# A spectral filter beside a gated MLP on one core: filter squares, a leftover row's chain and four butterflies stand elsewhere in the background list, and the last token block is split over two PSUM tiles

## Chip, core and metric

The kernel runs on one core of one Trainium2 chip. The metric is device time in microseconds, the median of several executions. Matmuls run on TensorE (PE), elementwise work on VectorE (DVE) and ScalarE (ACT), a few sums over partitions on GpSimd (POOL). Every DMA is issued from SyncE's queue (SP).

## What is computed

```python
xn = _layernorm(x, axis=-1)                      # x: 1 x 2048 x 448
return x + _A_ref(xn, A_w_r, A_w_i) + _B_ref(xn, B_W_gate, B_W_up, B_W_down)

def _A_ref(x, w_r, w_i):
    X = rfft2(x, axes=(-2, -1))                  # 2048 x 225
    X = X * (w_r + 1j * w_i)
    return irfft2(X, s=(S, D), axes=(-2, -1))

def _B_ref(x, W_gate, W_up, W_down):             # 448 -> 1792 -> 448
    gate = jnp.einsum("bsd,df->bsf", x, W_gate)
    up = jnp.einsum("bsd,df->bsf", x, W_up)
    h = gate * (gate > 0) * up
    return jnp.einsum("bsf,fd->bsd", h, W_down)
```

## The kernel before

The 2048 tokens stand as 16 blocks n2 of 128, four blocks to a chunk q of 512. Every f32 operand of a matmul is split into a high and a low float16 part, and a product is three matmuls (high by high, high by low, low by high) into one PSUM bank.

**The MLP is the foreground.** 56 `gu` units (14 slices f of the hidden dimension by 4 chunks) multiply the chunk by the slices of W_gate and W_up into a PSUM tile "gu" of two banks, of which there are two buffers. Units go in pairs: the last 64 input rows of both stand together as four half passes (L738), which also open the second unit's buffer. `gu_post` then follows on each unit: relu on ACT (L768, to g1), times up on DVE (L772), the high part on ACT (L776, to h), the low part on DVE (L780). A gu buffer is free when its L772 is through. `dn` units multiply h by W_down, block by block, into PSUM "dn" (two buffers, L799); DVE adds the result to the output tile xy (L805).

**The filter is the background.** The row DFT over d, the DFT over tokens (128 points by matmul, 16 points by four radix-2 stages on DVE), the product with the filter, and the way back. `stage2`, `stage3`, `stage4` are butterflies over tiles y of 128x456 (L404 to L428); with sign -1 they belong to the inverse. `i_swap`, `i_pair` and `i_quad` undo the pairing of frequencies (a swap of partitions by two DMAs, L529 and L530, into one of four tiles sw; L535 and L536; L602 to L607). `i_hi` and `i_lo` split into vt (L614 on ACT, L620 on DVE), `i_sdft` (L630) and `i_ddft` (L649) are the two inverse DFTs on PE into PSUM "fx" (two buffers), and `i_acc` (L654) adds to xy.

**The filter's scale and the leftover row.** The filter is scaled by a power of two taken from its sum of squares: `wsq` squares the 16 filter tiles on ACT (L186), `wneg` flips signs in them first (L496), `wsq_fin` sums them on DVE (L463) and over partitions on POOL (L189), `wsq_scale` makes the scale fsc on DVE (L192, L196, L470 to L472). Partition 64 of every tile holds two frequencies that don't fit the pairing. It is collected as a 16-row tile "row" and goes its own way: `row_hi`, `row_lo`, `row_dft(0)`, `row_mul`, then `row_hi2` (L566, ACT, needs fsc), `row_lo2` (L570, DVE), `row_dft(1)` (L575, PE), `row_ev` (L588, DVE). `i_swap` puts each row back into its block by a DMA (L592).

**What sets the order.** The foreground's units stand in a fixed list. The background is a list `bg` of items with a DVE cost; after each unit `run_bg` takes as many as the unit leaves room for on DVE. A scheduler then orders each engine's queue by its own model of time, so an item that moves in `bg` moves others on all engines. Each queue is fixed at build time, and each engine works through its queue in order: an instruction that waits holds up all behind it.

In `bg`, the loop over `i0` handles the inverse's first part: filter load, forward stage 4, pair, product (`wmul`), then `back`, which adds the inverse's first butterflies. The next loop, over t, handles one block of the inverse after another. `dn_tail` does the last four token blocks.

Of the kernel before, what the change touches and what calls it, by code (L numbers as in the profile page):

```python
# [10 lines left out]
F32 = mybir.dt.float32  # L11
# [3 lines left out]
OP = mybir.AluOpType  # L15
AX = mybir.AxisListType

S, D, F = 2048, 448, 1792
# [5 lines left out]
GROUPS = [5, 5, 4]  # L24
# [120 lines left out]
def tile_gfnet_reglu(ctx: ExitStack, tc: tile.TileContext, x, xr, wgu, wd, wf, ident, c_fd, c_fm, c_im, c_row, c_id,  # L145
                     out):
    nc = tc.nc
    V, A, P, G = nc.vector, nc.scalar, nc.tensor, nc.gpsimd

    main = ctx.enter_context(tc.tile_pool(name="main", bufs=1))  # L150
    psum = ctx.enter_context(tc.tile_pool(name="psum", bufs=1, space=bass.MemoryType.PSUM))

    def mt(shape, dt, name, bufs=1):
        return main.tile(shape, dt, name=name, bufs=bufs)

    def fx():
        return psum.tile([128, 512], F32, name="fx", bufs=2)
# [18 lines left out]
    dsc = mt([128, len(GROUPS)], F32, "dsc")  # L176
# [365 lines left out]
    def row_wf():  # L542
        w = state["roww"] = it([128, 2 * GW], F32, "roww")
        h = state["rowh"] = it([128, 2 * GW], F16, "rowh")
        G.memset(w[0:64], 0.0)
        G.memset(w[64:128], 0.0)
        G.memset(h, 0.0)
        for i in range(4):
            nc.sync.dma_start(w[32 * i:32 * i + 16], wf[:, 64, i // 2])
        A.activation(w[64:128, GW:2 * GW], w[64:128, GW:2 * GW], AF.Copy, scale=-1.0)  # L550

    def row_hi():
        h, t = state["rowh"], it([16, 4, KC], F16, "rowt")
# [18 lines left out]
    def row_dft(d):  # L572
        y = state["rowps"] = fx()[:, 0:2 * GW]
        for a in range(2):
            P.matmul(y, row_t[:, d, a], state["rowh"], start=(a == 0), stop=(a == 1), skip_group_check=True)  # L575
# [82 lines left out]
    wt, wdt, wsc = {}, {}, {}  # L658
# [61 lines left out]
    hps, ht = {}, {}  # L720
# [67 lines left out]
    dps = {}  # L788
# [18 lines left out]

    def dn_tail(fs, ns):

        ps = [psum.tile([128, 512], F32, name="dn", bufs=2) if i < 2 else fx() for i in range(4)]  # L810
        cut = [(slice(0, D),)] * 3 + [(slice(0, D // 2), slice(D // 2, D))]
        for end, p, n2, cs in [(False, p, n2, cut[0]) for p, n2 in zip(ps, ns)] + [(True, *e) for e in zip(ps, ns, cut)]:
            q, j = n2 % 4, n2 // 4
            js = slice(128 * j, 128 * (j + 1))
            for c in cs:
                for f in fs[-1:] if end else fs[:-1]:
                    for a, b in ((0, 0), (0, 1), (1, 0)):
                        P.matmul(p[:, c], ht[f, q][:, a, js], wdt[f][:, b, c],
                                 start=(not end and f == fs[0] and a + b == 0), stop=(end and a == 1),
                                 skip_group_check=True)  # L820
            dps[n2] = p
        for n2, cs in zip(ns, cut):
            for c in cs:
                V.scalar_tensor_tensor(xy[:, n2, c], dps[n2][:, c], dsc[:, len(GROUPS) - 1:len(GROUPS)], xy[:, n2, c],
                                       op0=OP.mult, op1=OP.add)
                nc.sync.dma_start(ov[:, n2, c], xy[:, n2, c])

    def store(n2):

# [10 lines left out]
    def add(cost, fn, *a):  # L840
        bg.append((cost, PE_US.get(fn.__name__, 0.0), fn, a))
# [15 lines left out]
    bf = (1.26, 2.04, 2.04, 2.04, 1.56, 2.04, 2.04, 2.04)  # L857
# [47 lines left out]
    add(0.0, lambda: nc.sync.dma_start(idc_t, c_id))  # L905
    ks = [0, 4, 2, 6, 1, 5, 3, 7]

    def back(k0):
        add(bf[0], inv1, k0)
        if k0 >= 4:  # L910
            for par in range(2):
                add(bf[4 * par], stage2, k0 - 4, par, -1, "i1", "i2")
            if k0 - 4 >= 2:
                for k in range(4):
                    add(bf[2 * k], stage3, k0 - 6, k, -1, "i2", "i3")

    rows = [lambda: (row_wf(), row_hi()), row_lo, lambda: row_dft(0), row_mul, row_hi2, row_lo2,
            lambda: row_dft(1), row_ev]
    rows_us = [0.0, 0.8, 0.0, 1.2, 0.0, 0.4, 0.0, 0.8]


    for i0 in range(10):
        if i0 < 8:
            k0 = ks[i0]
            for k in (k0, k0 + 8):
                add(0.0, load_wf, k)
            add(bf[k0], stage4, k0, 1, "s3", "X")
        pair_k = [k for k in ((ks[i0 - 2], ks[i0 - 2] + 8) if i0 > 1 else ())]
        for k in pair_k:
            add(0.78, pair, ("X", k), 1)  # L930
        if i0 < 8:
            for k in (k0, k0 + 8):
                add(0.0, swap, ("X", k))
        for k in (ks[i0 - 1], ks[i0 - 1] + 8) if 0 < i0 < 9 else ():
            add(0.0, wneg, k)
        for k in pair_k:
            add(2.04, wmul, k)
            add(0.0, wsq, k)
        if i0 > 1:
            back(ks[i0 - 2])  # L940
            if i0 - 2 < 4:
                add(rows_us[i0 - 2], rows[i0 - 2])
    add(0.1, wsq_fin)
    add(0.8, wsq_scale)
    for c, fn in zip(rows_us[4:], rows[4:]):
        add(c, fn)

    il = ((8, 0.68, i_acc), (6, 0.0, i_pq), (4, 0.69, i_lo), (6, 0.69, i_pqlo), (2, 0.78, i_pair), (2, 1.83, i_quad),
          (7, 0.0, i_ddft), (5, 0.0, i_sdft), (3, 0.0, i_hi), (0, 0.0, i_swap))
    io = [n for n0 in range(8) for n in (n0, n0 + 8)]  # L950
    for t in range(16 + 8):
        if t < 16 and t % 2 == 0:
            add(bf[t // 2], stage4, t // 2, -1, "i3", "U")
        if 3 <= t < 19:
            add(0.0, load_im, io[t - 3])
        for st, c, fn in il:
            if 0 <= t - st < 16:
                add(c, fn, io[t - st])
# [50 lines left out]
    def gslot(i, back):  # L1009
        n = gpos[i] - back  # L1010
        return gus[n] if n >= 0 else -1
# [48 lines left out]
    for c, q in enumerate(CHUNKS[:2]):  # L1060
# [3 lines left out]
        for j in range(4):  # L1064
            n2 = q + 4 * j
# [7 lines left out]
    q = CHUNKS[0]  # L1073
# [143 lines left out]
```

## Time and profile before

| | before |
|---|---|
| median of 3 runs (lowest to highest) | 449.18 us (448.53 to 449.6) |
| span of the profiled execution | 447.6 us |
| ACT busy | 186.7 us (42%) |
| POOL busy | 28.8 us (6%) |
| DMA, mean over the span | 88 GB/s |
| PE share of the chain that ended last | 52% |
| DVE share of it | 38% |

The profile is one execution, and times in it count from the span's start. The sign change, from forward to inverse, lies at about 300 us; the timeline shows POOL waiting until 302.7 us for the sum of the filter's squares (L189, out small). A group row of the timeline is: start, length, engine, line, operation, output and inputs, count, and in brackets the idle time before it and what ended it. In the chain of waits a row is: start, length, engine, tile, line, count, and successive rows show by their starts how far one instruction is from the next. DVE overlaps an instruction's end with the next one's start, so a row of the timeline is some 0.08 us longer than the step.

### The profile page before, as it was taken

What the parts mean: (1) busy time and instruction counts of PE and PEld (TensorE: products, weight loads), DVE (VectorE), ACT (ScalarE), POOL (GpSimd) and SP (SyncE); (2) the same over time, 40 slices, a digit from 0 to 9 for tenths busy, and PEclk for the clock granted to TensorE, in tenths of its full rate; (3) what the DMA queues carried; (4) which work ended last, traced back from release to release, by engine and by line L of the source; (5) the groups of instructions that cost most, each with busy time, mean ns of one, the idle gap of its engine ahead of it and who ended that gap; (6) DMA issues with size and microseconds to landing.
All of it is one profiled execution on the core that took longest, in us unless ns stands there. A gap on an engine that the chain in (4) does not pass through costs nothing.

```text
span 447.6 us, 7353 instructions
## 1 busy us (share of the span) xinstructions
PE 437.9 (98%) x2616; PEld 218.8 (49%) x2616; DVE 387.2 (87%) x958; ACT 186.7 (42%) x398; POOL 28.8 (6%) x77
## 2 busy tenths in 40 slices
PE   6999999999999999999999999999999999999996
PEld 2644645545445444444444444444445555555653
DVE  5999779777969998999999999999789799699753
ACT  5896263742553955133124255344214134134230
POOL 4220020200100140000000000000000000000000
PEclk9999999999999999999999999999999999999999
DMA  7828985400001272412220210001011211211212
GB/s 259 313 68 246 320 334 105 96 0 22 2 1 48 95 243 74 132 54 72 84 84 2 83 41 1 1 1 61 23 41 55 68 34 56 89 34 48 94 63 82
DMA packets 37756, 39.54 MB, mean 88 GB/s; under 512 B 16550, under 2 KB 33624, under 8 KB 37720
## 3 DMA queue, kind: packets, MB, share of 16 engines
q1 hardware_dynamic: 37720, 39.09, 28.0%
q8 instruction: 20, 0.33, 0.3%
q14 instruction: 16, 0.13, 0.1%
HBM read 24.38 MB, written 3.67 MB: 63 GB/s over the span
## 4 chain that ended last, share of the span: by engine, by line
PE 52%; DVE 38%; DMA 3%; issue 3%; ACT 2%; POOL 1%; SPq 1%; DVEq 0%; ACTq 0%; POOLq 0%
PE gu L731 26%; PE dn L799 12%; DVE g L772 3%; DVE h L780 3%; DVE wt L685 3%; DVE xy L805 2%; PE fx L630 2%; PE fx L649 2%; DVE y L502 2%; DVE y L503 2%; DVE y L405 2%; DVE y L404 2%; DMA sw<-y 2%; DVE y L427 2%; PE gu L738 2%
## 5 line engine op out<-in xcount | busy, mean ns | idle before, releaser
L731 PE MATMUL gu<-T,wt 128*128 128x512 f16 (+1 forms) x1140 | 255.0, 375 | 0.0
L731 PEld LDWEIGHTS <-wt 128*128 128x128 f16 x1140 | 108.8, 98 | 128.3 <-issue 8.5
L799 PE MATMUL dn<-wdt,h 128*128 128x448 f16 x624 | 127.1, 352 | 0.3 <-DVE xy L805 0.3
L799 PEld LDWEIGHTS <-h 128*128 128x128 f16 x624 | 60.3, 98 | 57.7 <-issue 1.1
L776 ACT ACTIVATE h<-g 128x512 f16<-128x512 f32 x56 | 35.0, 627 | 78.8 <-DVE g L772 78.6
L768 ACT ACTIVATE g<-gu 128x512 f32<-128x512 f32 x56 | 33.0, 589 | 73.7 <-PE gu L738 52.1
L772 DVE SCALAR_TENSOR_TENSOR g<-gu,g 128x512 f32<-128x512 f32 x56 | 38.2, 682 | 4.2 <-ACT g L768 4.2
L780 DVE TENSOR_TENSOR h<-g,h 128x512 f16<-128x512 f32 x56 | 38.2, 683 | 3.1 <-ACT h L776 2.6
L805 DVE SCALAR_TENSOR_TENSOR xy<-dn,dsc,xy 128x448 f32<-128x448 f32 x44 | 29.8, 678 | 6.2 <-PE dn L799 6.2
L614 ACT ACTIVATE vt<-y,fsc 128x456 f16<-128x456 f32 x16 | 10.8, 672 | 29.9 <-PE fx L630 17.4
L681 ACT ACTIVATE wt<-wst,wsc 128x512 f16<-128x512 f32 x28 | 19.0, 714 | 6.2 <-DVE wsc L196 6.2
L189 POOL PARTITION_ALL_REDUCE wm<-wm x15 | 9.3, 617 | 181.9 <-ACT junk L186 161.8
L654 DVE SCALAR_TENSOR_TENSOR xy<-fx,fsc,xy 128x448 f32<-128x448 f32 x16 | 10.9, 679 | 11.0 <-PE fx L649 10.9
L685 DVE SCALAR_TENSOR_TENSOR wt<-wst,wsc,wt 128x512 f16<-128x512 f32 x28 | 20.2, 744 | 0.1
L738 PE MATMUL gu<-T,wt 64*128 64x512 f16 x112 | 17.0, 381 | 1.6 <-DVE g L772 1.4
L535 DVE TENSOR_TENSOR y<-y,sw 128x228 f32<-128x228 f32 x32 | 12.4, 388 | 6.8 <-DMA sw<-y 4.1
L186 ACT ACTIVATE junk<-wst 128x512 bf16<-128x512 f32 x28 | 17.4, 622 | 1.3 <-DMA wst<-in_wgu 1.0
L405 DVE TENSOR_TENSOR y<-y,y 128x456 f32<-128x456 f32 x22 | 13.8, 628 | 1.7 <-DMA row<-y 1.4
L392 DVE TENSOR_TENSOR Xh<-X,Xh 128x456 f16<-128x456 f32 x16 | 9.9, 626 | 5.8 <-ACT Xh L389 5.7
L404 DVE TENSOR_TENSOR y<-y,y 128x456 f32<-128x456 f32 x22 | 13.8, 628 | 0.4
L630 PE MATMUL fx<-im,vt 128*128 128x128 f16 x192 | 13.5, 219 | 0.0
L389 ACT ACTIVATE Xh<-X 128x456 f16<-128x456 f32 x16 | 9.2, 577 | 10.1 <-DVE X L387 8.9
(128 smaller groups left out, 476.2 us busy)
## 6 DMA issues: line engine op xcount, KB each, us to landing
sw<-y SPq DMA_DIRECT2D x64, 112.2 KB
wst<-in_wgu SPq DMA_DIRECT2D x28, 256.0 KB
wf<-in_wf SPq DMA_DIRECT2D x16, 228.0 KB
y<-in_xr SPq DMA_DIRECT2D x16, 224.0 KB
xy<-in_x SPq DMA_DIRECT2D x16, 224.0 KB
out<-xy SPq DMA_DIRECT2D x15, 224.0 KB
wdst<-in_wd SPq DMA_DIRECT2D x14, 224.0 KB
fm<-in_c_fm SPq DMA_DIRECT2D x4, 256.0 KB
```

Source lines behind the costliest of these rows:

```text
L404: V.tensor_tensor(t, a, b, op=OP.add)
L405: V.tensor_tensor(b, a, b, op=OP.subtract)
L630: P.matmul(o, v[:, h, w], m[:, c, :], start=(i == 0), stop=(i == 2), skip_group_check=True)
L685: V.scalar_tensor_tensor(w[:, 4:8, :], st, sc, w[:, 0:4, :], op0=OP.mult, op1=OP.subtract)
L731: last["P"] = P.matmul(hps[f, q][:, g, cs], wt[f, g][:, a, :], Tq[q][:, b, cs], start=(start and i == 0), stop=(stop and i == len(seq) - 1 ...
L738: m = P.matmul(hps[f, q][:, g, 0:512], wt[f, g][rows, 7, :], Tq[q][rows, b, :], start=start, stop=not start).ins
L768: last["A"] = A.activation(g1s[f, q], hps[f, q][:, 0, :], AF.Relu, scale=2.0 ** -22).ins
L772: last["V"] = V.scalar_tensor_tensor(g1, hps[f, q][:, 1, :], 2.0 ** -22, g1, op0=OP.mult, op1=OP.mult).ins
L776: A.activation(ht[f, q][:, 0, :], g1s[f, q], AF.Copy)
L780: V.tensor_tensor(h[:, 1, :], g1s.pop((f, q)), h[:, 0, :], op=OP.subtract)
L799: last["P"] = P.matmul(ps[:, 0:D], ht[f, q][:, a, js], wdt[f][:, b, :], start=(i == 0), stop=(i == n - 1)).ins
L805: last["V"] = V.scalar_tensor_tensor(xy[:, n2, :], dps[n2][:, 0:D], dsc[:, g:g + 1], xy[:, n2, :], op0=OP.mult, op1=OP.add).ins
```

## The change

Three edits.

- In the `i0` loop, `wsq(k)` stands right behind `wneg(k)`, one round of the loop ahead of `wmul(k)`. `wsq_fin` therefore can be added at `i0 == 8`, and `wsq_scale` and the last four steps of the leftover row (`rows[4:]`) are added in turns of two, behind the two products and behind `inv1` of the last round (`i0 == 9`). Before, all of these stood behind the loop.
- The four `stage3` butterflies of j = 1 leave `back` and are added one at a time at t = 0, 2, 4, 6 of the block loop.
- `dn_tail` takes the third block's PSUM from a gu buffer instead of fx, and does the last block as two halves of 224 columns in two tiles (a gu buffer and an fx one): all products of the first half, then all of the second. Before, one tile held the block, the products of all but the last f ran at full width, and only the last f was cut in two.

```diff
     def dn_tail(fs, ns):
-        ps = [psum.tile([128, 512], F32, name="dn", bufs=2) if i < 2 else fx() for i in range(4)]
-        cut = [(slice(0, D),)] * 3 + [(slice(0, D // 2), slice(D // 2, D))]
-        for end, p, n2, cs in [(False, p, n2, cut[0]) for p, n2 in zip(ps, ns)] + [(True, *e) for e in zip(ps, ns, cut)]:
+        gu = [psum.tile([128, 2, 512], F32, name="gu", bufs=2) for _ in range(2)]
+        ps = [*(psum.tile([128, 512], F32, name="dn", bufs=2) for _ in range(2)), gu[0][:, 0]]
+        parts = [(p, n2, slice(0, D)) for p, n2 in zip(ps, ns)]
+        two = [(p, ns[3], slice(h * D // 2, (h + 1) * D // 2)) for h, p in enumerate((gu[1][:, 0], fx()))]
+        for end, (p, n2, c) in [(e, u) for us in (parts, two[:1], two[1:]) for e in (False, True) for u in us]:
...
-        for n2, cs in zip(ns, cut):
-            for c in cs:
-                V.scalar_tensor_tensor(xy[:, n2, c], dps[n2][:, c], dsc[:, len(GROUPS) - 1:len(GROUPS)], xy[:, n2, c],
-                                       op0=OP.mult, op1=OP.add)
-                nc.sync.dma_start(ov[:, n2, c], xy[:, n2, c])
+        for p, n2, c in parts + two:
+            V.scalar_tensor_tensor(xy[:, n2, c], p[:, c], dsc[:, len(GROUPS) - 1:len(GROUPS)], xy[:, n2, c],
+                                   op0=OP.mult, op1=OP.add)
+            nc.sync.dma_start(ov[:, n2, c], xy[:, n2, c])
...
-    def back(k0):
+    def back(k0, late):
         add(bf[0], inv1, k0)
+        for c, fn in late:
+            add(c, fn)
         if k0 >= 4:
             for par in range(2):
                 add(bf[4 * par], stage2, k0 - 4, par, -1, "i1", "i2")
-            if k0 - 4 >= 2:
+            if k0 == 6:
                 for k in range(4):
-                    add(bf[2 * k], stage3, k0 - 6, k, -1, "i2", "i3")
+                    add(bf[2 * k], stage3, 0, k, -1, "i2", "i3")
...
         for k in (ks[i0 - 1], ks[i0 - 1] + 8) if 0 < i0 < 9 else ():
             add(0.0, wneg, k)
+            add(0.0, wsq, k)
+        late = [(0.8, wsq_scale), *zip(rows_us[4:], rows[4:])] if i0 == 9 else []
         for k in pair_k:
             add(2.04, wmul, k)
-            add(0.0, wsq, k)
+            for c, fn in late[:2]:
+                add(c, fn)
+            late = late[2:]
+        if i0 == 8:
+            add(0.1, wsq_fin)
         if i0 > 1:
-            back(ks[i0 - 2])
+            back(ks[i0 - 2], late)
             if i0 - 2 < 4:
                 add(rows_us[i0 - 2], rows[i0 - 2])
-    add(0.1, wsq_fin)
-    add(0.8, wsq_scale)
-    for c, fn in zip(rows_us[4:], rows[4:]):
-        add(c, fn)
...
     for t in range(16 + 8):
+        if t < 8 and t % 2 == 0:
+            add(bf[t], stage3, 1, t // 2, -1, "i2", "i3")
         if t < 16 and t % 2 == 0:
             add(bf[t // 2], stage4, t // 2, -1, "i3", "U")
```

How the queues move shows at three places. First DVE, around the L772 of the unit whose g1 is g_3279 before and g_3289 after, at 284.5 us of the profile before; eg and wsc are scales of gate and up weights, wt their float16 parts, y the filter's tiles. Before:

```order
L404 TENSOR_TENSOR y_77<-y_72,y_79 128x456
L772 SCALAR_TENSOR_TENSOR g_3279<-gu,g_3279 128x512
L192 TENSOR_SCALAR eg<-wm 128x2
L405 TENSOR_TENSOR y_79<-y_72,y_79 128x456
L404 TENSOR_TENSOR y_72<-y_75,y_77 128x456
L780 TENSOR_TENSOR h<-g_3279,h 128x512
L805 SCALAR_TENSOR_TENSOR xy<-dn,dsc,xy 128x448
L685 SCALAR_TENSOR_TENSOR wt<-wst,wsc,wt 128x512 x2
L192 TENSOR_SCALAR eg<-wm 128x2
L405 TENSOR_TENSOR y_77<-y_75,y_77 128x456
L805 SCALAR_TENSOR_TENSOR xy<-dn,dsc,xy 128x448
```

And the same place in the changed kernel:

```order
L404 TENSOR_TENSOR y_77<-y_72,y_79 128x456
L405 TENSOR_TENSOR y_79<-y_72,y_79 128x456
L805 SCALAR_TENSOR_TENSOR xy<-dn,dsc,xy 128x448
L685 SCALAR_TENSOR_TENSOR wt<-wst,wsc,wt 128x512 x2
L192 TENSOR_SCALAR eg<-wm 128x2
L588 TENSOR_SCALAR row<-fx,small 16x4x57 x2
L404 TENSOR_TENSOR y_72<-y_75,y_77 128x456
L196 TENSOR_SCALAR wsc<-eg 128x2
L805 SCALAR_TENSOR_TENSOR xy<-dn,dsc,xy 128x448
L192 TENSOR_SCALAR eg<-wm 128x2
L405 TENSOR_TENSOR y_77<-y_75,y_77 128x456
L772 SCALAR_TENSOR_TENSOR g_3289<-gu,g_3289 128x512
```

The row's last step (L588) has come up here from behind the unit at 311 us, and the L772 has gone down behind it and behind ten instructions that used to follow.

Second SP, where the inverse's blocks begin: y is a block of the inverse, row the leftover row's tile, sw a swap's tile.

```order
-L529 DMA sw_1906<-y_75 63x456
-L530 DMA sw_1906<-y_75 63x456
-L529 DMA sw_1907<-y_85 63x456
-L530 DMA sw_1907<-y_85 63x456
-L592 DMA y_77<-row 1x12x38
-L592 DMA y_79<-row 1x12x38
-L592 DMA y_75<-row 1x12x38
-L592 DMA y_85<-row 1x12x38
 L592 DMA y_74<-row 1x12x38
 L529 DMA sw_1904<-y_74 63x456
 L530 DMA sw_1904<-y_74 63x456
+L592 DMA y_79<-row 1x12x38
```

Before, the swaps of the first four blocks (eight DMAs) go ahead of five row DMAs; now each block's row DMA stands ahead of its own swap.

Third the end of DVE's queue, the last four blocks:

```order
 L654 SCALAR_TENSOR_TENSOR xy<-fx,fsc,xy 128x448 x2
-L824 SCALAR_TENSOR_TENSOR xy<-dn,dsc,xy 128x448 x2
-L824 SCALAR_TENSOR_TENSOR xy<-fx,dsc,xy 128x448
-L824 SCALAR_TENSOR_TENSOR xy<-fx,dsc,xy 128x224 x2
+L823 SCALAR_TENSOR_TENSOR xy<-dn,dsc,xy 128x448 x2
+L823 SCALAR_TENSOR_TENSOR xy<-gu,dsc,xy 128x448
+L823 SCALAR_TENSOR_TENSOR xy<-gu,dsc,xy 128x224
+L823 SCALAR_TENSOR_TENSOR xy<-fx,dsc,xy 128x224
```

The order of the steps is the same; the third block and the last one's first half now come from gu buffers.

More of the change, by code (lines that the diff above doesn't have):

```diff
@@ L808, in dn_tail @@
     def dn_tail(fs, ns):
-        ps = [psum.tile([128, 512], F32, name="dn", bufs=2) if i < 2 else fx() for i in range(4)]
-        cut = [(slice(0, D),)] * 3 + [(slice(0, D // 2), slice(D // 2, D))]
-        for end, p, n2, cs in [(False, p, n2, cut[0]) for p, n2 in zip(ps, ns)] + [(True, *e) for e in zip(ps, ns, cut)]:
+        gu = [psum.tile([128, 2, 512], F32, name="gu", bufs=2) for _ in range(2)]
[3 more added lines that the diff above has]
+        for end, (p, n2, c) in [(e, u) for us in (parts, two[:1], two[1:]) for e in (False, True) for u in us]:
             q, j = n2 % 4, n2 // 4
             js = slice(128 * j, 128 * (j + 1))
-            for c in cs:
[L816 to L821, printed above, removed]
-        for n2, cs in zip(ns, cut):
-            for c in cs:
-                V.scalar_tensor_tensor(xy[:, n2, c], dps[n2][:, c], dsc[:, len(GROUPS) - 1:len(GROUPS)], xy[:, n2, c],
-                                       op0=OP.mult, op1=OP.add)
-                nc.sync.dma_start(ov[:, n2, c], xy[:, n2, c])
+            for f in fs[-1:] if end else fs[:-1]:
+                for a, b in ((0, 0), (0, 1), (1, 0)):
+                    P.matmul(p[:, c], ht[f, q][:, a, js], wdt[f][:, b, c],
+                             start=(not end and f == fs[0] and a + b == 0), stop=(end and a == 1),
+                             skip_group_check=True)
+        for p, n2, c in parts + two:
+            V.scalar_tensor_tensor(xy[:, n2, c], p[:, c], dsc[:, len(GROUPS) - 1:len(GROUPS)], xy[:, n2, c],
+                                   op0=OP.mult, op1=OP.add)
+            nc.sync.dma_start(ov[:, n2, c], xy[:, n2, c])
     def store(n2):
```

## The prediction

> **What bounds the kernel now.** I read the page first, then the busy time by stretch, then the waits of PE alone, then the chain and the timeline around each wait. The profiled execution spans 447.6 us; the median of the runs shown is 449.18 us, 1.6 us more, which lies outside the span.
>
> ```profile
> span 447.6 us, 7353 instructions
> ...
> PE 437.9 (98%) x2616; PEld 218.8 (49%) x2616; DVE 387.2 (87%) x958; ACT 186.7 (42%) x398; POOL 28.8 (6%) x77
> ```
>
> PE shows 98% busy, but matmul ends are modelled, so I check that against the distance from one matmul to the next. In the chain of waits, 20 products of 512 columns take 4.32 us, 0.216 us each, and 24 of 448 columns take 4.54 us, 0.189 us each. Both are the same 0.42 ns a column.
>
> ```profile
> 337.21 4.32 PE gu L731 x20
> ...
> 342.20 4.54 PE dn L799 x24
> ```
>
> In the page's 40 slices PE stands at nine tenths or more in all but the first and the last, and by 20 us only two stretches between the opening and the end have a gap:
>
> ```profile
> PE   6999999999999999999999999999999999999996
> ...
> 300.00:320.00 20.00, 19.71 (x99) 8.76 (x97) 17.04 (x48) 6.36 (x11) 0.47 (x1) 1.00 0.15 46
> 320.00:340.00 20.00, 18.60 (x100) 9.04 (x100) 18.38 (x49) 5.90 (x10) 0.00 (x0) 1.00 0.08 24
> ```
>
> The columns are PE, PEld, DVE, ACT, POOL, granted clock, DMA share, GB/s. So PE is the bound nearly everywhere, at a granted clock of 1.00, and time can come only from the 1.7 us without PE here, from the opening, which the change leaves alone, or from what follows the last matmul. The waits of PE name who ended the two gaps:
>
> ```profile
> PE gu L738 <- DVE g L772: 1.4, 1, 1.4
> ...
> PE dn L799 <- DVE xy L805: 0.3, 1, 0.3
> ```
>
> The idle figures leave out modelled ends, so I take the gaps from starts. First gap: a group of four half passes (L738) is normally followed by the next group 0.53 us after its start (307.52 to 308.05); here by 0.89 us (319.07 to 319.96). That is 0.36 us lost.
>
> ```profile
> 307.52 0.60 PE L738 MATMUL gu<-T,wt 64*128 64x512 f16 x4
> 308.05 0.82 PE L731 MATMUL gu<-T,wt 128*128 128x512 f16 x3
> ...
> 319.07 0.60 PE L738 MATMUL gu<-T,wt 64*128 64x512 f16 x4
> 319.96 0.54 PE L799 MATMUL dn<-wdt,h 128*128 128x448 f16 x2 [0.29 <-DVE xy L805]
> ```
>
> Second gap: six L630 products take 0.35 us (336.70 to 337.05), so those at 334.27 are through at 334.62; with 0.1 us for the change of form the half passes could start at 334.7, and start at 336.16. That is 1.46 us lost, 1.82 together.
>
> ```profile
> 334.27 0.50 PE L630 MATMUL fx<-im,vt 128*128 128x128 f16 x6
> 336.16 0.61 PE L738 MATMUL gu<-T,wt 64*128 64x512 f16 x4 [1.40 <-DVE g L772]
> 336.70 0.51 PE L630 MATMUL fx<-im,vt 128*128 128x128 f16 x6
> 337.05 0.81 PE L731 MATMUL gu<-T,wt 128*128 128x512 f16 x3
> ```
>
> DVE was late both times, and it was late because it had stood still: 2.65 us for the leftover row's way back into U (L592), 1.42 us for a swap. The times step (L772) whose end frees the gu buffer stands behind both.
>
> ```profile
> 315.92 0.40 DVE L535 TENSOR_TENSOR y<-y,sw 128x228 f32<-128x228 f32 x1 [2.65 <-DMA y<-row]
> ...
> 329.45 0.40 DVE L535 TENSOR_TENSOR y<-y,sw 128x228 f32<-128x228 f32 x1 [1.42 <-DMA sw<-y]
> ...
> 335.43 0.68 DVE L772 SCALAR_TENSOR_TENSOR g<-gu,g 128x512 f32<-128x512 f32 x1
> ```
>
> **The row's chain.** The row is written about 23 us earlier on DVE, and each row DMA now stands ahead of its own block's swap in SP's queue instead of behind eight swaps. The first row DMA is then released by the butterfly that makes its block, not by the row. Between that butterfly and the pair step that waited 2.65 us now stand 17 DVE instructions, among them two L772, seven butterfly steps of 228 or 456 columns and a weight split: some 6 us, against 4.2 us for row DMA and swap (below). That wait goes. With it the L805 that PE waited for at 319.96 is over 1.5 us early, so the first gap goes: -0.36.
>
> What is late next is the price of the move: DVE does this work ahead of a times step that had room before. In the order of the changed kernel the L772 that frees the buffer (g_3289, formerly g_3279) stands behind work that used to follow it. In steps of the chain:
>
> ```profile
> 284.62 0.60 DVE g L772
> ...
> 285.30 0.55 DVE y L405
> ...
> 285.87 0.63 DVE y L404
> ...
> 287.11 0.59 DVE xy L805
> 287.70 1.32 DVE wt L685 x2
> ...
> 302.54 0.08 DVE small L463
> ...
> 307.47 0.46 DVE rowh L570
> ...
> 311.74 0.35 DVE row L588
> ...
> 312.10 0.46 DVE row L588
> ```
>
> Moved ahead of it: two L405 (1.10), an L404 (0.63), two L805 (1.18), the L685 pair (1.32) and three small ones at 0.08, 4.47 us; from the row, two L588 (0.81), L570 (0.46) and six scale steps at 0.08 (0.48), 1.75 us. So L772 starts at 284.6 + 6.2 = 290.8 and, at 0.68 long, ends at 291.5. PE wants the buffer later as well:
>
> ```profile
> 285.92 8.80 PE L731 MATMUL gu<-T,wt 128*128 128x512 f16 x40
> ```
>
> The second unit of these 40 starts 20 x 0.216 after 285.92, at 290.24. Ahead of it now come six dn products (6 x 0.189 = 1.13) and the row's two products of 228 columns (0.2 by their columns), which makes 291.57. So L772 is just in time, with 0.1 us to spare by this sum; dependent DVE steps that stand alone cost 0.63 and interleaved ones 0.55 (the L404 and L405 above), and the new order interleaves more, which gives some tenths back. I take a stall of 0, bounded by 0 and 0.6. The next three L772 (g_3336, g_3387, g_3430) have the same instructions ahead of them as before but for a few, where PE had no wait.
>
> [...]
>
> **The four butterflies.** Four of the eight third-stage butterflies move from 293 to 305 us to between 297 and 331. DVE does the same work; by the L772 of the second gap the two orders have done the same number of instructions, one apart. New is where a swap is waited for: block 2's pair step stands 2.1 us of DVE work behind the butterfly that feeds it (L603, L428, L604, L605, L772, L606, L607), and the row DMA, two swap issues and the landing take
>
> ```profile
> 325.12 0.71 SPq L592 DMA_DIRECT2D y<-row  x1
> ...
> 326.65 2.68 DMA sw<-y
> ```
>
> from 325.12 to 329.33, 4.2 us. So DVE waits about 2.1 us there, where it waited 1.42 before. Behind the waiting instruction stand an L805, a weight split, two L620 and the L772 that PE's half passes need. That L772 comes at 335.43 - 2.65 - 1.42 + 2.1 = 333.5 and ends at 334.2. PE, without its two gaps, reaches the half passes at 334.7 - 0.36, plus six more L630 (0.35) and three dn products (0.57) that now stand ahead: 335.3. Spare 1.1 us, so the second gap goes: -1.46. The first L630 moves a unit ahead in PE's order. Its operand was ready at 322.4 even behind DVE's long wait, and PE wants it 20 x 0.216 after 325.63 less 0.36, at 329.6, so that costs nothing.
>
> ```profile
> 321.70 0.69 DVE L620 SCALAR_TENSOR_TENSOR vt<-y,fsc,vt 128x456 f16<-128x456 f32 x1
> ...
> 325.63 8.80 PE L731 MATMUL gu<-T,wt 128*128 128x512 f16 x40
> ```
>
> **The squares.** ACT does the same 16 squares, now behind their sign flips; where two stand together ahead of an h copy, that copy is a square later. ACT is 42% busy, and the copy has a DVE queue ahead of its reader. If that cover fails, DVE waits for part of a square, inside the 0.6 above.
>
> **The tail.** Both halves' L824 used to start after the last matmul, since one tile held both, and the second store followed the first on SP.
>
> ```profile
> 443.82 0.81 DVE L824 SCALAR_TENSOR_TENSOR xy<-fx,dsc,xy 128x224 f32<-128x224 f32 x2 [1.59 <-PE fx L818]
> ...
> 444.30 0.81 SPq L826 DMA_DIRECT2D out<-xy  x2
> ```
>
> Now twelve matmuls of 224 columns (0.096 each, 1.15 us) follow the first half's last one, so its L824 and its store (0.4 each) are done before the second half ends. The second half's store is issued where the first one's was: 0.81 / 2 = 0.40 earlier. PE does 18 products of 224 columns for 9 of 448: 18 x 0.096 - 9 x 0.189 = +0.03. The third block and the first half take gu buffers, whose last reader is the times step of the last unit; PE does 18 dn products (3.4 us) and two more groups between that unit and them, so no wait is added. Sum -0.37; bounds 0 (the first half still waits) and -0.45.
>
> **Sum.** -0.36 - 1.46 - 0.37 = -2.19 on 447.6, that is 445.4 of span, and 447.0 us on the median. After 340 us PE never waited and DVE comes nearer on time than before, so nothing is given back there.
>
> **Rivals.** (1) DVE late at the moved L772, the stall above: 0.3 to 1.5 us, for it the 0.1 us of spare, against it that the interleaving gives back; 447.3 to 448.5, about 447.8. (2) The swap's wait is longer than 4.2 us by over 1.1 and the second gap returns in its new place; only the first gap and the tail are won: 449.18 - 0.73 = 448.4. For it, the wait exists in the order; against it, SP's queue holds nothing else then. (3) Slower: the second row DFT (L575) now stands between two dn blocks at 282.4 us, and everything on PE waits behind it. It needs the all-sum, six small DVE steps, an ACT copy queued behind four squares, and L570. L570 stands where DVE was at
>
> ```profile
> 280.52 0.62 DVE L503 TENSOR_TENSOR y<-y,wf 128x456 f32<-128x456 f32 x1
> ```
>
> and with 0.4 for five scale steps ends at 281.4. PE is there at 285.92, less 30 dn products (5.67) and the half passes (0.63), plus 15 products (2.84): 282.4, 1 us later. Should the copy miss its place on ACT and the chain come 4.2 us late, PE stalls 3.2 and the time is 450.2; from 3.2 us late on the change loses. Against it: ACT and POOL are mostly idle, and the squares ahead of the copy need only loads that lie in the past. (4) The tail's halves still wait for each other: 447.4.
>
> **How the numbers follow.** Forecast 0.70, rival 1 0.14, rival 2 0.09, rival 3 0.04, rival 4 0.03. A measurement here tells about 0.2%, 0.9 us, from no change: faster is below 448.28, slower above 450.08. Faster: 0.69 of the forecast, rival 4, 0.11 of rival 1, 0.01 of rival 2: 0.84. Same: 0.01, 0.03 and 0.08 of those: 0.12. Slower: rival 3, 0.04. The range runs from 446.3 (the forecast with some tenths that the interleaving gives, and the spread of the runs) to 448.4 (rivals 1 and 2 for the most part).
>
> **What would show it.** PE without a wait for L805 or L772 between 290 and 340; DVE's 2.65 us for the row gone, one wait of about 2 us for a swap left near 322; L772 at 290 to 291 just ahead of its unit; two stores at the end over 1 us apart. Wrong would be a PE wait for DVE near 291 or 335, PE waiting at L575, or L823 for the first half starting with the second.

## The result, and the profile after

| | before | after |
|---|---|---|
| median (lowest to highest), 6 runs each | 449.4 us (448.53 to 450.53) | 446.78 us (446.59 to 447.5) |
| span of the profiled execution | 447.6 us | 445.7 us |
| half passes at 267 us to half passes at 425 us | 159.14 us | 157.33 us |
| start of the first eviction behind the last matmul to the end of the span | 3.78 us | 3.22 us |

The ratio is 0.9944, 95% interval 0.9932 to 0.9956: the changed kernel is 2.0 to 3.1 us faster. The forecast was 447.0 us, in a range of 446.3 to 448.4.

First the page of the kernel after: PE's busy time is within 0.2 us of what it was (437.9), the span is shorter.

```profile
span 445.7 us, 7367 instructions
...
PE 438.1 (98%) x2625; PEld 219.4 (49%) x2625; DVE 386.9 (87%) x958; ACT 187.0 (42%) x398; POOL 27.7 (6%) x77
```

Then the waits of PE after. The two rows of the gaps, L772 with 1.4 and L805 with 0.3, are gone, and what is left lies in the first 20 us.

```profile
PE dn L1054 <- POOL warm L1111: 3.6, 1, 3.6
PE fx L332 <- ACT wt L681: 0.5, 1, 0.5
PE gu L738 <- DVE wt L685: 0.2, 1, 0.2
```

The busy time of the two stretches that had the gaps, after (PE, PEld, DVE, ACT, POOL, clock, DMA share, GB/s). PE fills both; DVE, which stood still in the first of them, now does so in the second.

```profile
300.00:320.00 20.00, 20.00 (x98) 8.76 (x96) 19.79 (x53) 7.15 (x12) 0.00 (x0) 1.00 0.15 46
320.00:340.00 20.00, 20.00 (x109) 9.61 (x108) 17.55 (x46) 4.78 (x8) 0.00 (x0) 1.00 0.09 28
```

The rows of the timeline after, on the places that the prediction named.

```profile
264.91 0.41 POOL L189 PARTITION_ALL_REDUCE wm<-wm  x1 [4.71 <-ACT junk L186]
266.17 1.40 POOL L189 PARTITION_ALL_REDUCE small<-small  x1 [0.86 <-DVE small L463]
266.30 0.39 DVE L536 TENSOR_TENSOR y<-y,sw 128x228 f32<-128x228 f32 x1
266.61 0.39 DVE L535 TENSOR_TENSOR y<-y,sw 128x228 f32<-128x228 f32 x1
267.26 0.61 PE L738 MATMUL gu<-T,wt 64*128 64x512 f16 x4
...
281.13 0.45 DVE L570 SCALAR_TENSOR_TENSOR rowh<-rowv,fsc,rowh 48x228 f16<-48x228 f32 x1
282.88 0.36 PE L575 MATMUL fx<-rowh,row_t 128*128 128x228 f16 x2
...
290.87 1.30 PE L799 MATMUL dn<-wdt,h 128*128 128x448 f16 x6
291.18 0.68 DVE L772 SCALAR_TENSOR_TENSOR g<-gu,g 128x512 f32<-128x512 f32 x1
292.00 4.48 PE L731 MATMUL gu<-T,wt 128*128 128x512 f16 x20
...
325.79 0.40 DVE L535 TENSOR_TENSOR y<-y,sw 128x228 f32<-128x228 f32 x1 [2.32 <-DMA sw<-y]
333.62 0.69 DVE L772 SCALAR_TENSOR_TENSOR g<-gu,g 128x512 f32<-128x512 f32 x1
335.70 0.60 PE L738 MATMUL gu<-T,wt 64*128 64x512 f16 x4
...
424.59 0.61 PE L738 MATMUL gu<-T,wt 64*128 64x512 f16 x4
...
441.33 0.45 DVE L823 SCALAR_TENSOR_TENSOR xy<-gu,dsc,xy 128x224 f32<-128x224 f32 x1 [0.42 <-PE gu L819]
442.48 0.45 DVE L823 SCALAR_TENSOR_TENSOR xy<-fx,dsc,xy 128x224 f32<-128x224 f32 x1 [0.70 <-PE fx L819]
442.96 0.33 SPq L825 DMA_DIRECT2D out<-xy  x1
```

At the half passes of 267 us this execution is 0.44 us later than the one of before (267.26 against 266.82; where that comes from is taken up at the end of the account below), so 0.44 goes off each time of after in the middle. The L772 that had moved down starts at 291.18, the next unit on PE at 292.00, with no wait. One wait for a swap is left, 2.32 us. The L772 of the second gap comes 2.1 us before its half passes. The last two evictions lie 1.15 us apart.

The kernel before, the two groups of half passes that bound the stretch in the table:

```profile
266.82 0.61 PE L738 MATMUL gu<-T,wt 64*128 64x512 f16 x4
...
425.96 0.60 PE L738 MATMUL gu<-T,wt 64*128 64x512 f16 x4
```

425.96 - 266.82 = 159.14 before, 424.59 - 267.26 = 157.33 after: 1.81 us less. This stretch serves below as the measure of the middle edits. The measure of the tail is the time from the start of the last eviction to the end of the span; where two evictions follow the last matmul, as in the kernel before, it counts from the first of them. The first measure repeats to 0.04 us over kernels with the same middle, the second to 0.1 over kernels with the same tail, since the page gives the span to 0.1 us.

### The profile page after: what moved, and what is told of

Its sections match the earlier page's. It is cut to its first block, busy times and chain, and to the rows that moved or that the text cites. A ratio compares the mean times of both kernels' runs of the same rounds, so it can differ in the third digit from the quotient of the medians.

```text
span 445.7 us, 7367 instructions
## 1 busy us (share of the span) xinstructions
PE 438.1 (98%) x2625; PEld 219.4 (49%) x2625; DVE 386.9 (87%) x958; ACT 187.0 (42%) x398; POOL 27.7 (6%) x77
## 4 chain that ended last, share of the span: by engine, by line
PE 79%; DVE 9%; DMA 5%; ACT 3%; issue 1%; SPq 1%; DVEq 0%; ACTq 0%
PE gu L731 44%; PE dn L799 22%; PE gu L738 3%; PE fx L630 2%; PE fx L649 2%; PE fx L361 2%; PE fx L398 2%; DMA wf<-in_wf 1%; DMA sw<-y 1%; DMA y<-in_xr 1%; ACT junk L186 1%; PE dn L819 1%; ACT wt L681 1%; PE gu L819 1%; DVE wt L685 1%
## 5 line engine op out<-in xcount | busy, mean ns | idle before, releaser
L772 DVE SCALAR_TENSOR_TENSOR g<-gu,g 128x512 f32<-128x512 f32 x56 | 38.3, 684 | 4.2 <-ACT g L768 4.1
L805 DVE SCALAR_TENSOR_TENSOR xy<-dn,dsc,xy 128x448 f32<-128x448 f32 x44 | 29.9, 679 | 6.3 <-PE dn L799 6.2
L189 POOL PARTITION_ALL_REDUCE wm<-wm x15 | 7.8, 518 | 179.6 <-ACT junk L186 175.5
L535 DVE TENSOR_TENSOR y<-y,sw 128x228 f32<-128x228 f32 x32 | 12.5, 390 | 5.0 <-DMA sw<-y 4.9
```

Source lines behind the costliest of these rows:

```text
L772: last["V"] = V.scalar_tensor_tensor(g1, hps[f, q][:, 1, :], 2.0 ** -22, g1, op0=OP.mult, op1=OP.mult).ins
L805: last["V"] = V.scalar_tensor_tensor(xy[:, n2, :], dps[n2][:, 0:D], dsc[:, g:g + 1], xy[:, n2, :], op0=OP.mult, op1=OP.add).ins
```

## The experiments

The theory: PE is the bound, and the gain is the two PE gaps that DVE's standing still had made (1.82 us), and an earlier last store. Rivals: the gain comes from one edit alone; each middle edit has its own gap; the times step at 291 us isn't as tight as the sum made it. All ratios are to the kernel before on the same chip; the table holds what the runs gave, and the text after it what each tells.

| run | ratio, 95% interval | median | 267 to 425 us | last eviction to end |
|---|---|---|---|---|
| tail_only | 0.9988 (0.9977 to 1.0) | 448.56 | 159.10 | 3.21 |
| middle_only | 0.9962 (0.9949 to 0.9974) | 447.78 | 157.33 | 3.82 |
| row_only | 0.9964 (0.995 to 0.9978) | 447.53 | 157.34 | 3.74 |
| butterflies_only | 0.9975 (0.9965 to 0.9985) | 448.38 | 157.89 | 3.78 |
| no_row_back | 0.9973 (0.9963 to 0.9983) | 448.04 | 157.66 | 3.84 |
| row_and_tail | 0.9957 (0.9944 to 0.9969) | 447.21 | 157.33 | 3.23 |
| tail_one_tile | 0.9963 (0.9951 to 0.9976) | 447.47 | 157.32 | 3.81 |
| tail_uneven | 0.9955 (0.9943 to 0.9968) | 447.21 | 157.32 | 3.07 |
| dose_first | 1.0095 (1.0073 to 1.0118) | 454.2 | 164.53 | 3.20 |
| dose_small | 1.0002 (0.9992 to 1.0011) | 449.16 | 159.19 | 3.27 |
| dose_second | 0.9967 (0.9957 to 0.9978) | 447.96 | 157.70 | 3.25 |
| row_lo_later | 0.9957 (0.9942 to 0.9972) | 447.47 | 157.40 | 3.05 |

### The tail alone, and the middle alone

tail_only is the kernel before with the new `dn_tail`:

```diff
     def dn_tail(fs, ns):
-        ps = [psum.tile([128, 512], F32, name="dn", bufs=2) if i < 2 else fx() for i in range(4)]
+        gu = [psum.tile([128, 2, 512], F32, name="gu", bufs=2) for _ in range(2)]
...
```

> The kernel before with the new last block (two halves in two PSUM tiles) and nothing else. Theory: the tail is worth 0.4 to 0.55 us, since the second half's store is issued 0.40 earlier after the last matmul; both PE gaps (0.36 at 319, 1.46 at 335) stay. Span 447.1 to 447.2, median 0.4 to 0.5 below the kernel before's. Rival (most of the gain is the tail): over 1 us. Rival (the halves still wait for each other): within 0.1 us, and the first half's L823 starts with the second's.

The stretch is 159.10, so both gaps stayed. The last eviction starts 3.21 us before the end where before it was 3.78: 0.57 us won. The median says 0.5 (449.27 x 0.0012), with an interval from 0 to 1.0.

middle_only is the changed kernel with the old `dn_tail`, the same lines the other way round.

> The changed kernel with the old last block: squares, row's chain and butterflies moved, tail as before. Theory: both PE gaps go, 1.82 us, and the tail shows its two stores 0.40 apart again: span about 445.8, median 1.8 below the kernel before's. Rival (something besides the two gaps and the tail was won, since the medians are 2.6 apart where the sum was 2.2): over 2.1 us.

157.33: 1.81 us won in the middle, none in the tail (3.82). The two parts, 1.81 and 0.57, add up to 2.38, and the stretches of the changed kernel show just these two (1.81 and 0.56).

### One middle edit at a time

row_only has the squares and the row's chain moved, and keeps the old `dn_tail` and the butterflies' old place. Against the changed kernel the butterflies go back like this:

```diff
-            if k0 == 6:
+            if k0 - 4 >= 2:
                 for k in range(4):
-                    add(bf[2 * k], stage3, 0, k, -1, "i2", "i3")
+                    add(bf[2 * k], stage3, k0 - 6, k, -1, "i2", "i3")
...
-        if t < 8 and t % 2 == 0:
-            add(bf[t], stage3, 1, t // 2, -1, "i2", "i3")
```

> Squares and row's chain moved, the four butterflies left at their old place, old tail. Theory as the prediction had it (each edit has its own gap): the row's 2.65 us wait and the first gap go, 0.36 us, the second gap is still there because a swap is waited for ahead of its L772: median 0.4 below. Rival (shared slack: both gaps come from one lateness of DVE, which stood still 2.65 + 1.42 us): without the 2.65 the L772 of the second gap is early enough too, both gaps go, 1.8 us.

Both gaps are gone (157.34). The expectation that followed the prediction's own division, 0.4 us, fell; shared slack stands. The timeline of row_only shows the place of the second gap, and a wait at 193 us that is spoken of further down:

```profile
193.11 4.48 PE L731 MATMUL gu<-T,wt 128*128 128x512 f16 x20 [0.51 <-DVE g L772]
...
334.39 0.68 DVE L772 SCALAR_TENSOR_TENSOR g<-gu,g 128x512 f32<-128x512 f32 x1
335.49 0.61 PE L738 MATMUL gu<-T,wt 64*128 64x512 f16 x4
```

The times step starts 1.10 us before the half passes. In the changed kernel it is 2.08, so the butterflies' move bought another us of lead, which PE has no use for.

butterflies_only is the other half: the kernel before with `stage3` of j = 1 in the block loop (the lines above with their signs turned), and nothing else.

> The four butterflies moved into the block loop, squares and row's chain left behind the loop over i0, old tail. With 8 butterfly steps a side out of its way the row's chain itself comes earlier by its place in the background list (its L588 some 15 us earlier on DVE). Theory as the prediction had it: the second gap goes, 1.46, the first one (row) only if the chain is early enough: 1.5 to 1.8 us. Rival (shared slack): the row's wait of 2.65 us goes too and both gaps with it, 1.8 us, so that the two middle edits alone are worth as much as both together. Rival (the row's second DFT now comes late on PE): a wait of PE at L575 and a smaller gain.

It takes both old gaps too, since the row's chain comes earlier by itself. But a new one shows at 303 us, in the timeline of butterflies_only:

```profile
302.22 1.30 PE L799 MATMUL dn<-wdt,h 128*128 128x448 f16 x6
303.17 0.69 DVE L772 SCALAR_TENSOR_TENSOR g<-gu,g 128x512 f32<-128x512 f32 x1
303.91 4.48 PE L731 MATMUL gu<-T,wt 128*128 128x512 f16 x20 [0.40 <-DVE g L772]
```

Six products of 0.189 from 302.22 end at 303.35; PE starts at 303.91: 0.56 us lost, 159.14 - 1.82 + 0.56 = 157.88. The row's last two steps (L588, at 296.05 and 297.26, 0.85 us of DVE together) now stand ahead of this times step. It starts 0.95 us behind the six products, where in the kernel before it is 0.08 (301.86 against 301.78); the 0.87 fits the two steps, though other steps moved as well. That is the first rival of the prediction, at another place. The row rival (PE waiting at L575) did not come.

### The wait itself taken away

no_row_back is the kernel before without the row's DMA into U; no item of the background list is moved.

```diff
     def i_swap(n2):
-        nc.sync.dma_start(cur["U", n2][64:65], row[n2:n2 + 1])
         swap(("U", n2))
```

> The kernel before without the row DMAs into U (L592), so the leftover row isn't put back; every step stays in its place on DVE and PE but for a few neighbours. Shared slack (DVE's standing still for the row delays every later times step): the 2.65 us wait is gone, the first gap (0.36) with it, and the L772 of the second gap, 2.65 us earlier, ends near 333.5, before PE wants it: both gaps go, 1.8 us, median 447.5. Rival (the butterflies' place makes the second gap by itself, through the swap that is waited for): only the first gap goes, 0.4 us, median 448.9.

With the butterflies at their old place and only neighbours reordered by the planner from 312 us on, 1.48 of the 1.82 us are gone (157.66). The timeline of no_row_back:

```profile
326.34 0.40 DVE L535 TENSOR_TENSOR y<-y,sw 128x228 f32<-128x228 f32 x1 [2.30 <-DMA sw<-y]
...
335.35 0.61 PE L738 MATMUL gu<-T,wt 64*128 64x512 f16 x4 [0.26 <-DVE g L772]
```

DVE's 4.07 us of waiting (2.65 + 1.42) has become 2.30, and the second gap 0.34 in place of 1.46. It is DVE's lateness, and not the place of the butterflies, that made both gaps; a part of the lead went to a longer wait for the next swap.

### The butterflies left out of the change

row_and_tail is row_only with the new `dn_tail`.

> The changed kernel with the four butterflies left at their old place. Shared slack: the row's move alone takes both gaps and the tail is worth 0.4 to 0.55, so this is the changed kernel's time: 446.7 to 447.0, 2.3 to 2.6 us below the kernel before's. Rival (the butterflies' move adds something of its own): slower than the changed kernel by 0.3 us or more.

157.33 and 3.23, the changed kernel's own two numbers. The medians (447.21 and 446.78, ratios 0.9957 and 0.9944 with overlapping intervals) don't separate them. The four butterflies' move brought nothing that these runs can see.

### One tile for the last block, and an uneven cut

tail_one_tile keeps the new order of the products and puts both halves into one tile:

```diff
-        two = [... for h, p in enumerate((gu[1][:, 0], fx()))]
+        two = [... for h, p in enumerate((gu[1][:, 0],) * 2)]
```

> The changed kernel with both halves of the last block in one PSUM tile, the new order of its products kept. Theory (one tile holds the first half back): the first half's L823 starts with the last matmul's end, beside the second half's, the second store is 0.40 later, and the stretch from the start of the last matmul to the end of the span is 3.9 to 4.1 us as before, where the changed kernel has 3.5. Rival (the order of the products makes the gain): 3.5 us, first half's L823 over 1 us ahead.

The timeline of tail_one_tile:

```profile
441.89 0.81 DVE L823 SCALAR_TENSOR_TENSOR xy<-gu,dsc,xy 128x224 f32<-128x224 f32 x2 [1.57 <-PE gu L819]
442.37 0.81 SPq L825 DMA_DIRECT2D out<-xy  x2
```

Both evictions start after the last matmul, and the end is 3.81 us away as before (3.78; the expectation counts from the last matmul's start, some 0.3 us earlier). So the tile holds the first half back, not the order. Whether a first half in a shared tile could be drained while PE still writes the second is not shown: no run here tried it.

tail_uneven cuts at column 288:

```diff
-        two = [(p, ns[3], slice(h * D // 2, (h + 1) * D // 2)) for h, p in enumerate((gu[1][:, 0], fx()))]
+        two = [(p, ns[3], c) for c, p in zip((slice(0, 288), slice(288, D)), (gu[1][:, 0], fx()))]
```

> The changed kernel with the last block cut at column 288 in place of 224. Theory (what follows the last matmul is one L823 of the last part and one store): the last L823 goes from 0.45 to about 0.35 us for 160 columns, the first part's L823 and store still fit beside the last part's 12 products of 0.068 (0.81 us): the last stretch is 0.1 us shorter, 3.4, and the median the same within 0.2. Rival (the first part's store is still on SP): no gain or 0.1 longer.

The timeline of tail_uneven:

```profile
441.50 0.52 DVE L823 SCALAR_TENSOR_TENSOR xy<-gu,dsc,xy 128x288 f32<-128x288 f32 x1 [0.74 <-PE gu L819]
442.33 0.38 DVE L823 SCALAR_TENSOR_TENSOR xy<-fx,dsc,xy 128x160 f32<-128x160 f32 x1 [0.31 <-PE fx L819]
442.75 0.33 SPq L825 DMA_DIRECT2D out<-xy  x1
```

The eviction is 0.07 shorter, its store is issued 0.42 after its start (0.48 in the changed kernel), and the end is 3.07 us away, 0.15 less. The median can't show that (447.21).

### More work ahead of the times steps

dose_first puts three more steps ahead of the L772 at 291 us (this edit and the next are written out over lines here; in the kernel each is one line):

```diff
     def gu_times(f, q):
         g1 = g1s[f, q]
+        for _ in range(3 if (f, q) == (6, 3) else 0):
+            V.tensor_tensor(g1, g1, g1, op=OP.max)
```

> The changed kernel with three more steps on DVE (g1 is replaced by the maximum of itself and itself, 0.60 us each, 1.8 in all) right ahead of the times step whose end frees the gu buffer at 291 us, the one that the prediction gave 0.1 us of spare; the order of PE ahead of that place is the same. In the changed kernel's trace L772 starts at 291.18, and where PE waits for such a step it starts 0.74 after it, so the spare is 292.00 - 291.92 = 0.08. Theory (DVE is just in time there): PE stalls 1.7 us at 291.9 with L772 as the releaser, and none of it comes back: the stretch from the half passes at 267 to those at 425 goes from 157.3 to 159.0 us, the median 1.7 above the changed kernel's. Rival (the buffer isn't what PE needs next, or DVE has hidden slack): under 0.5 us.

The stretch grew by 7.2 us, not 1.7. Two things were missed. The timeline of dose_first:

```profile
291.59 1.30 PE L799 MATMUL dn<-wdt,h 128*128 128x448 f16 x6
291.91 0.69 DVE L771 TENSOR_TENSOR g<-g 128x512 f32<-128x512 f32 x1
...
296.34 0.68 DVE L772 SCALAR_TENSOR_TENSOR g<-gu,g 128x512 f32<-128x512 f32 x1
297.07 7.33 PE L731 MATMUL gu<-T,wt 128*128 128x512 f16 x20 [4.19 <-DVE g L772]
304.34 0.61 PE L738 MATMUL gu<-T,wt 64*128 64x512 f16 x4
```

The planner put butterflies and weight splits between the three, so that the first times step of the pair starts at 296.34 where it would have started at 291.91: 4.43 late. PE was free at 291.59 + 6 x 0.189 = 292.72 and started at 297.07: 4.35 lost. The difference, 0.08, is the spare. And the 20 products behind it take 7.27 us (297.07 to 304.34) where 20 x 0.216 and 0.1 for the change of form make 4.42 (4.41 in before, 314.66 to 319.07). The busy time by stretch of dose_first gives the granted clock there and on either side:

```profile
290.00:297.00 7.00, 2.88 (x15) 1.27 (x13) 6.97 (x17) 3.15 (x5) 0.00 (x0) 0.93 0.00 0
297.00:302.60 5.60, 5.53 (x14) 1.89 (x14) 5.60 (x15) 2.20 (x4) 0.00 (x0) 0.50 0.00 0
302.60:306.00 3.40, 3.40 (x18) 1.26 (x17) 2.59 (x8) 0.89 (x2) 0.00 (x0) 0.96 0.24 73
```

A clock of 0.93 over the first 7 us is 1.0 us at half, and 0.96 over the last 3.4 is 0.3 us: by these three shares the clock was at half from about 296.0 to 302.9, an estimate. By it the clock had fallen 3.3 us after PE ran out of products (292.72). PE worked at half the clock for 5.8 us (297.07 to 302.9), in which the trace has products 0.427 us from start to start in place of 0.216. 7.27 - 4.42 = 2.85, and 4.35 + 2.85 is the 7.2. A gap of 4.35 us was followed by this here, gaps of 1.46 us (before) and 1.86 us (next run) were not, and no run has one between them behind PE's first product. The price differs from one execution to the next: three of the four have a mean granted clock of 0.991 or 0.992 and spans of 452.3 to 453.6 us, the fourth has 0.996 and 450.6.

dose_small has one such step, into a scratch tile:

```diff
         g1 = g1s[f, q]
+        if (f, q) == (6, 3):
+            V.tensor_tensor(it([128, 512], BF16, "late"), g1, g1, op=OP.max)
```

> The changed kernel with one more step on DVE (0.60 us, the maximum of g1 with itself, into a scratch tile) ahead of the times step at 291 us. Between it and that times step the planner now also puts an exponent step, two butterfly steps of 228 columns and a weight split (0.07 + 0.31 + 0.66 + 0.31), so that L772 comes 1.95 us late; PE's order up to there is unchanged. Theory (PE pays for lateness there beyond 0.07 us of spare, one for one, and full speed returns at once): PE stalls 1.88 us, the matmuls behind it keep their 0.216 us, the stretch from the half passes at 267 to those at 425 us is 159.2 where the changed kernel has 157.3. Rival (what the run with three steps showed, where a stall of 4.35 us was followed by 13 products at 0.427 us in place of 0.216, comes with any stall): 159.2 and 2.7 more, 161.9. Rival (the stall is made up later): 157.3 to 158.

159.19 us, as the theory had it. The timeline of dose_small:

```profile
290.85 1.30 PE L799 MATMUL dn<-wdt,h 128*128 128x448 f16 x6
293.10 0.68 DVE L772 SCALAR_TENSOR_TENSOR g<-gu,g 128x512 f32<-128x512 f32 x1
293.84 4.49 PE L731 MATMUL gu<-T,wt 128*128 128x512 f16 x20 [1.69 <-DVE g L772]
```

PE was free at 291.98 and started at 293.84, 1.86 lost for 1.95 of lateness, and the products behind keep their speed (4.49 for 20). So PE's gain in the middle rests here on a spare of 0.1 us.

dose_second is dose_first's edit at the second gap's times step, (f, q) = (13, 0).

> The same 1.8 us on DVE ahead of the times step of the second gap (L772 starts at 333.62 in the changed kernel, PE wants its buffer at 335.70, 1.3 us of spare); the planner moves 15 dn products (2.84 us) ahead of the half passes that need it, so that the spare is 4.2. Theory (it is lateness against PE's need and not DVE's load that costs): no gap at the half passes, 0 to 0.3 us in all. Rival (DVE is as much a bound as PE in this stage, so that any work added on it shows): 1 us and more.

The timeline of dose_second:

```profile
334.06 0.69 DVE L771 TENSOR_TENSOR g<-g 128x512 f32<-128x512 f32 x1
...
335.63 3.57 PE L799 MATMUL dn<-wdt,h 128*128 128x448 f16 x18
338.76 0.69 DVE L772 SCALAR_TENSOR_TENSOR g<-gu,g 128x512 f32<-128x512 f32 x1
339.51 0.61 PE L738 MATMUL gu<-T,wt 64*128 64x512 f16 x4 [0.31 <-DVE g L772]
```

The same three steps cost 0.37 us (157.70) where they had cost 7.2. Here too the planner pushed other work between them: the times step starts at 338.76 where it would have started at 334.06, 4.70 late. PE was free at 335.63 + 18 x 0.189 + 0.1 = 339.13, so that the spare was 4.3, where 4.2 was worked out, and 0.38 were lost. In these two runs DVE's load is not what PE pays for; lateness beyond the spare is.

### An attempt at a better version

row_lo_later takes tail_uneven and moves the row's low split one round later:

```diff
-            if i0 - 2 < 4:
-                add(rows_us[i0 - 2], rows[i0 - 2])
+            for r in {2: (0,), 4: (1, 2), 5: (3,)}.get(i0, ()):
+                add(rows_us[r], rows[r])
```

> The changed kernel with the last block cut at 288 and with the leftover row's low split (L562, L563, 0.82 us on DVE) one round later. Every trace so far has the same order up to 250 us, and shows between 0 and 0.8 us lost where PE waits for the L772 behind those two steps at 192 us, and up to 0.3 at 204. Theory (that L772 is as much just in time as the one at 291): the gap at 192 is gone, the stretch from 267 to 425 us stays 157.3, the last stretch 3.3, span 444.5 to 445.2, median 446.3 to 446.9: the fastest of all by 0 to 0.5. Rival (the lateness at 192 comes from a swap's landing and not from the two steps): the gap shows there still, or at the next L772, and the median is that of the kernel with the uneven cut, 447.2.

No gap shows at 192 us, and one of 0.35 us came at a later tight times step. The timeline of row_lo_later:

```profile
222.72 4.48 PE L731 MATMUL gu<-T,wt 128*128 128x512 f16 x20 [0.18 <-DVE g L772]
```

The ratio, 0.9957, is no better than tail_uneven's 0.9955. What the rival forecast came, a gap at a later L772 and no gain; its cause is not shown. Nor is it shown that the move took the gap at 192: the traces of before, after, tail_one_tile and tail_uneven have none there either. And the expectation was wrong that every trace has the same order up to 250 us: with the row's chain moved the queues differ from 162 us on, ACT's first (the squares).

## Why the prediction was right, point by point

- **PE is the bound, and the two gaps go.** The middle gave 1.81 us where 1.82 was worked out, in six kernels that have the row's chain moved without added work (157.32 to 157.34; row_lo_later has 157.40). PE's busy time changed by 0.2 us.
- **The moved L772.** Predicted start 290.8, PE's need 291.57. Measured, with 0.44 off: 290.74 and 291.56. The two doses put the spare at 0.1 us. The stall of 0 was the right choice in its range of 0 to 0.6. That it came out within 0.1 us of a stall, as the sum said, is also luck: the times of the steps in the sum aren't known that finely.
- **The second gap.** Predicted end of its L772 334.2, PE's need 335.3; measured 333.87 and 335.26. The swap's wait was 2.32 us where 2.1 was worked out.
- **Which edit wins the second gap: wrong.** The step "so the second gap goes: -1.46" stands under the four butterflies, and only 0.36 under the row. The row's move alone takes both gaps (row_only), as the step's own term of 2.65 us implied: lateness of DVE is one account, and either edit alone pays off most of it. The total was right because the two were never counted twice; the division was not, and a learner who had kept only the butterflies' edit for its 1.46 us would have won 1.25 (159.14 - 157.89).
- **The squares.** The all-sum took 1.40 us on POOL at 266.17, and the steps of two SBUF operands beside it (L535 and L536, four of them from 266.00 to 267.22) stand 0.30 to 0.31 us apart from start to start, as the same steps do from 259.85 on. So DVE was not held up, and the sum was right to have no term for it. Why the all-sum took longer here than its 0.47 us in the kernel before (302.71) is not shown. Two others took 0.41: one beside an L772, which reads PSUM (after, 264.91), and one in before at 258.73, beside which an L502 of two SBUF operands starts at 259.01 and takes 0.62. The 1.40 us cost nothing, since the scale is made on DVE only from 276.6 us on.
- **The second row DFT.** L570 ended at 281.58, PE came to L575 at 282.88: 1.3 us to spare where 1.0 was worked out. The slower rival had no opening.
- **The tail: mis-sized.** -0.40 predicted from the last eviction on (with 0.03 more for PE, -0.37, and a bound of -0.45), -0.56 measured. The second store's issue starts 0.43 earlier, about as worked out: the trace of before has the two issues at 0.33 and 0.38 us, so the second starts at 445.11 - 0.38 = 444.73, 0.91 after the evictions do, and after it is 0.48 (442.96 - 442.48). Of the other 0.13 the sum had nothing. 0.05 is the issue, 0.38 us right behind another and 0.33 alone. 0.08 lies behind its end (2.51 us to the end of the span before, 2.43 after): the last packets end 0.98 and 0.97 after the issue, and then SyncE has one closing semaphore step fewer, 0.06. tail_one_tile, which differs in the tiles alone, has all of it back (3.81).
- **The median.** The sum of the stretches is 2.37 us, the medians lie 2.6 apart, and kernels with the same middle and no worse a tail came out 2.2 below (449.43 - 447.21) and, row_lo_later, 1.9. So the forecast's nearness to the median, 0.2 us, is in part chance. What blurs the medians lies ahead of the two gaps: the first half passes start between 19.09 and 20.05 us in these traces, and at 192 and 204 us, where a tight times step and an h copy stand, PE loses between 0 and 0.8 and between 0 and 0.5 us from one execution to the next. The changed kernel's profiled execution lost 0.15 in the opening and 0.29 by 227 us to the one before, the 0.44 above. Whether the change has a part in it stays open, since its queues differ from 162 us on. From the first half passes to those at 267 us the four traces with the old order take 247.1 to 248.0 us and the nine with the new one 247.0 to 248.2; that shows no cost of the change there and can't exclude one of some tenths.

## What to carry to other kernels

Where one engine bounds and another feeds it just in time, look for the places where the feeding engine stands still, not for its busy share: 4 us of standing still made both gaps, and each of three edits that removed the first wait took the first gap and most of the second (the row's move all of it; no_row_back left 0.34 us, butterflies_only opened another gap of 0.56). Count lateness as one account over the whole queue, and test each edit by itself before crediting it with a gap. A result that was to be drained in pieces needed a PSUM tile for each piece here (3.81 us to the end with one tile for both halves, 3.22 with two), and a smaller last piece took 0.15 us more off the tail.

## What the runs showed of the hardware that was not expected

- In dose_first a gap of 4.35 us on PE was followed by some 5.8 us of work at a granted clock of 0.50 (512 columns in 0.427 us), so that a stall of 4.35 us cost 7.2 in the profiled execution. Gaps of 1.46 and 1.86 us (before, dose_small) cost only themselves.
- A store's issue on SyncE right behind another took 0.38 us (before, tail_one_tile) and 0.33 where it stood alone (after); from the second issue's start to the end of the span it is 2.90 us in before and 2.77 in after.
- POOL's all-sum of the squares took 1.40 us beside four unbroken DVE steps of two SBUF operands (after), and 0.47 in before.
- PE starts 0.73 to 0.75 us after the start of the DVE step that it waits for (0.68 us long), in butterflies_only and the three runs with added steps alike.
